# Global value rows of half batches 2 to 5: fetched by one gather and small transfers instead of picked by matmuls

## The chip, the cores and the metric

The kernel runs on one core of one Trainium2 chip. The metric is the device time of one execution in microseconds (us); less is better. The numbers come from a profile of one execution and from three timed runs.

## The reference

Eight batches, eight heads, 576 tokens, head size 64. Each token attends to a band of 32 tokens on either side and to eight global tokens, whose rows and columns are full. The attention output goes through a two-layer network with a cosine gate.

```python
scores = scale * np.matmul(q, k.transpose(0, 1, 3, 2))
mask = np.abs(pos[:, None] - pos[None, :]) <= window          # window = 32
mask = mask | is_global[:, None] | is_global[None, :]
scores = np.where(mask, scores, -1000000000.0)
attn = softmax(scores)                                        # over the last axis
attn_out = np.matmul(attn, v)
x = attn_out.transpose(0, 2, 1, 3).reshape(B * S, H * D)      # 4608 x 512
h = x @ w_in                                                  # 512 x 2048
out = (h * np.cos(h)) @ w_out                                 # 2048 x 512
```

## The kernel before, in words

Work is cut into 16 half batches of four heads, and each of these into two pairs of heads (pair `pr`, 0 to 31). The network is cut into nine blocks of 512 tokens. Every engine runs its instructions in the order in which they are recorded, and that order is written out by hand as strings of steps. `FRONT` covers the first five half batches (pairs 0 to 9) and the first matmuls of the network; `MID`, `FIFTH`, `SIXTH` and `ORDER` cover the rest, in which attention is mixed into the network's matmuls.

In a step's name a digit is a pair or a half batch. In `FRONT`, `k` and `q` turn a pair's keys and queries on TensorE and copy them out on ScalarE (L604, L615, L616); `s` is a pair's scores, exponentials and mask (L631 on TensorE, L634 and L638 on ScalarE, L635 and L639 on VectorE); `p` multiplies with the values and normalizes (L646 on TensorE, L660 to L666 on VectorE); `x` turns the result (L678, L679 to L684); `f` issues filler matmuls that nobody reads (L493); `m` and `t` are the network's first matmuls (L762) and cosines; `n` squares a half batch's result on ScalarE (L818); `H1` turns the gathered global keys and queries on TensorE and copies them on VectorE (L555, L557), and `g` spreads them on GpSimd.

For the first five half batches the values lie in natural layout. `M` clears part of a buffer `vn` on VectorE (L378) and issues five loads from SP's queue (L373), for five windows of 120 rows. Partitions 0 to 7 are kept for the eight global tokens; GpSimd clears them early on (`clear_rows`, L383). `C` casts the buffer to fp16 on GpSimd (L402) into the buffer `vw`, behind a gate, a one-element copy that waits for the mask product of the newest pair recorded so far (L400). `y` then picks a pair's eight global rows out of the cast windows with five matmuls against a 0/1 matrix (L409), and ScalarE copies them into partitions 0 to 7 of all five windows (L410). The buffer of half batch 4 is that of half batch 2, so the clearing of `M4` on VectorE waits for the cast `C2` on GpSimd.

SP's queue numbers its transfers round robin over eight semaphores: a transfer is issued only when the one eight places earlier has landed. GpSimd's queue has its own eight.

Of the kernel before, what the change touches and what calls it, by code (L numbers as in the profile page):

```python
# [17 lines left out]
B, H, S, D = 8, 8, 576, 64  # L18
# [5 lines left out]
G = 8  # L24
# [7 lines left out]
NK5 = 5  # L32
# [9 lines left out]
C = G + QB  # L42
# [10 lines left out]

SIXTH = "sa 2 2 2 2 sz pa 1 1 2 xa pz G 1 1 2 xz n 1 1 D0 2 kc qc D1 1 D2 2 1"

FRONT = ("M1 s0 E0 C0 E1 L2 w6 k1 q1 w4 s1 y0.0 f8 k2 q2 C1 H0 p0 M2 L3 y0.1 s2 k3 q3 f6 x0 p1 M3 H1 g4 g5 g6 C2 y1.0 s3 g7 L4 I k4 q4 f6 x1 p2 M4 y1.1 s4 "
         "C3 W0 k5 q5 f6 x2 p3 y2.0 s5 g8 g9 W1 W2 W3 k6 q6 f6 x3 p4 y2.1 s6 C4 Y0 k7 q7 f6 x4 p5 n0 y3.0 s7 k8 q8 f6 x5 p6 y3.1 s8 H2 k9 q9 f6 x6 p7 y4.0 s9 "
         "x7 p8 y4.1 O m m x8 K5 p9 t t + m m t t x9 -")
WARM = 13
OK_ALL = float(P * (B * NP * 2 * BP + B))  # L60

# [1 line left out]
def view(ap, *dims):  # L63

    return bass.AP(ap.tensor, ap.offset, [ap.ap[0], *[list(d) for d in dims]])


def dview(ap, offset, *dims):

    return bass.AP(ap.tensor, ap.offset + offset, [list(d) for d in dims])  # L70
# [134 lines left out]
def kernel(  # L205
# [10 lines left out]
    nc = tc.nc  # L216
# [46 lines left out]
    def cast_half(s, which):  # L263

        base = s * 4 * S * D
        for x in which:
            if x == "v":
                nc.gpsimd.dma_start(v16[s * 4 * S : (s + 1) * 4 * S].rearrange("(n r) d -> n (r d)", r=16),
                                    dview(v, base, (16 * D, 4 * S // 16), (1, 16 * D)))
            else:  # L270
                src, dst = {"k": (k, k16), "q": (q, q16)}[x]
                nc.gpsimd.dma_start(dst[s].rearrange("t (h d) -> t h d", h=4),  # L272
                                    dview(src, base, (D, S), (S * D, 4), (1, D)))

    def load_qk(s, hs=(0, 4)):

        base = (s * 4 + hs[0]) * S * D
        for src, dst in ((k, kn[s % NN][KPAD : KPAD + S // RW]), (q, qn[s % NN][0 : S // RW])):
            nc.gpsimd.dma_start(dst[:, hs[0] : hs[1]].rearrange("x h r d -> x h (r d)"),
                                dview(src, base, (RW * D, S // RW), (S * D, hs[1] - hs[0]), (1, RW * D)))  # L280
# [9 lines left out]
    vg32 = keep.tile([P, 2, 2, D], FP32)  # L290
# [24 lines left out]
    def warm(n, tag="s"):  # L315

        t = ps.tile([P, 4, P], FP32, tag=tag, bufs=2 + (tag == "s"))
        for _ in range(n):
            nc.tensor.matmul(t, ones16, view(ones16, (0, 4), (1, P)), start=True, stop=True)  # L319

    p8 = keep.tile([P, 1], FP32)
# [10 lines left out]
    def gather(src, dst, half):  # L332
        rows = src.rearrange("b h s d -> (b h s) d")
        for h in range(2):
            nc.gpsimd.indirect_dma_start(
                out=dst[:, half, h], out_offset=None, in_=rows,
                in_offset=bass.IndirectOffsetOnAxis(ap=gidx_rows[:, 0:1], axis=0),
                element_offset=(half * 32 + h) * S * D)
# [23 lines left out]
    def vn_of(s):  # L362
        i = s if s < 4 else 2
        return view(vn32[i // 2][:, 4 * (i % 2)], (4 * D, NK5), (1, 4 * D))

    def load_vn(s, t0=0, t1=NK5):

        rows = vn_of(s)
        for t in range(t0, t1):
            lo = max(KS * t - 24, 0)  # L370
            n = min(KS * t + 96, S) - lo
            p0 = G + (24 if t == 0 else 0)
            nc.sync.dma_start(rows[p0 : p0 + n, t].rearrange("p (h d) -> p h d", h=4),  # L373
                              dview(v, (s * 4 * S + lo) * D, (D, n), (S * D, 4), (1, D)))
# [3 lines left out]
        nc.vector.memset(vn_of(s)[0:64, 0], 0.0)  # L378
        load_vn(s)

    def clear_rows(s):

        nc.gpsimd.memset(vn_of(s)[0:G, 1:], 0.0)  # L383

    gate = keep.tile([1, 1], FP16)

# [367 lines left out]
    def mlp_in(t, f):  # L754
        if f == 0:
            g_of[t] = work.tile([P, NF, TT], FP16, tag="g", name="g")
        g16 = g_of[t]
        tag = "s" if spare[0] and f % 4 > 1 else "h"
        ph = ps.tile([P, TT], FP32, tag=tag, bufs={"s": 3, "h": 2}[tag], name="ph")
        ph_of.append((ph, g16[:, f]))  # L760
        for j in range(NC):
            nc.tensor.matmul(ph, w_in16[:, j, f * P : (f + 1) * P], xT[:, j, t * TT : (t + 1) * TT],  # L762
                             start=(j == 0), stop=(j == NC - 1))

    def mlp_act():
        ph, g = ph_of.pop(0)
        cos = work.tile([P, TT], FP16, tag="cos", bufs=3)
        nc.scalar.activation(cos, ph, AF.Sin, bias=pio2)  # L768
        nc.vector.tensor_tensor(g, cos, ph, ALU.mult)  # L769
# [99 lines left out]
    def one(act=True):  # L869
        for _ in range(1):  # L870

            if ins_q and ins_q[0][0] < ready[0] and ins_q[0][0] < outs_q[0][0] + 2:
                t, f = ins_q.pop(0)
                mlp_in(t, f)
                if act:
                    mlp_act()
                ready[1] = t * NF + f + 1
# [22 lines left out]
    with tc.manual_schedule():  # L900
# [21 lines left out]
        build_band()  # L922
        index_rows(1)
        load_vn(0)
        for s in range(1, 4):
            clear_rows(s)
        load_qk(1)
        build_ones()
        build_mask5()
# [60 lines left out]
            load_values(2 * s)  # L990
            load_values(2 * s + 1)

        def late_gathers(_):

            gather(v, vg32, 0)

        LOCAL = {"k": local_k, "q": local_q}
        OTHER = LOCAL | {"g": globals_kq, "L": load_qk, "W": load_w_in, "v": load_values, "n": x_squares,
                 "C": cast_vn, "I": row_numbers, "E": early_rows, "w": lambda n: warm(n, "h" if n == 6 else "s"), "y": value_rows, "M": next_values, "N": clear_rows, "Y": late_gathers, "V": hold, "U": hold_x, "H": early_globals, "Z": steady_buffers, "f": fill, "r": load_vn, "A": later_rows, "D": later_globals, "O": load_w_out, "K": lambda s: cast_half(s, "vkq"), "B": bring, "m": lambda _: one(False), "t": lambda _: mlp_act()}
        ready[0] = 1  # L1000
        for step in FRONT.split():
            if step in "+-":
                spare[0] = step == "+"
                continue
            f = (STEPS | OTHER)[step[0]]
            f(*[int(x) for x in (step[1:] or "0").split(".")])
        ready[0], front[0] = 2, False
        for s in range(4, B * NP // 2):
            outs_by[0] = 8 * (s - 3)
            for step in {4: MID, 5: FIFTH, 6: SIXTH}.get(s, ORDER).split():  # L1010
# [20 lines left out]
                else:  # L1031
                    f, pr = (STEPS | OTHER)[step[0]], 2 * s + "azcd".index(step[1])
# [56 lines left out]
```

## Time and profile before

| | before |
|---|---|
| median of 3 runs | 351.18 us (351.07 to 353.2) |
| profiled execution | 349.19 us, span 347.3 us |
| TensorE busy | 329.4 us (95%) |
| VectorE busy | 249.5 us (72%) |
| ScalarE busy | 246.0 us (71%) |
| GpSimd busy | 110.0 us (32%) |
| granted TensorE clock, mean | 0.99 |

The span runs from the first to the last instruction; the execution's own time is 1.89 us longer, and its time is 0.6% below the median of the runs. Matmuls overlap, so a busy TensorE is not one at its peak. In the rows below, the time in square brackets is how long an engine stood idle before the instruction, and behind the arrow is what ended the wait. L numbers are lines of the kernel before; the change moves most lines by one.

### The profile page before, as it was taken

To read this page: it belongs to the slowest core of one execution; us is meant where nothing else is said; L and a number is where in the kernel's file an instruction comes from. 1 tells how busy PE (TensorE), PEld (TensorE's weight loads), DVE (VectorE), ACT (ScalarE), POOL (GpSimd) and SP (SyncE) were. 2 spreads that over 40 slices of the span, in tenths; PEclk is the share of its full clock that TensorE was granted. 3 is DMA by queue.
4 is the path that set the end of the run, shared out by engine and by line. 5 is a ranking of instruction groups with operands and counts; after the bars stand their busy time and mean duration, and the time that the engine had idled before them with its cause. 6 is when DMAs were issued, how large, how long until landed. Compare 5 with 4: busy or idle time off the path is not lost.

```text
span 347.3 us, 8464 instructions
## 1 busy us (share of the span) xinstructions
PE 329.4 (95%) x3207; PEld 172.7 (50%) x3207; DVE 249.5 (72%) x611; ACT 246.0 (71%) x423; POOL 110.0 (32%) x221
## 2 busy tenths in 40 slices
PE   7977989999989999999999999999999999999993
PEld 3566865444445454545454545454545344444442
DVE  6665778987597688888797878788888466556310
ACT  8878797796566896878787777878787866644300
POOL 8754846632352506050705062325001000000000
PEclk9999899999999999999999999999999999999997
DMA  5998992999999999999999999999990001100112
GB/s 78 185 165 152 171 195 39 187 175 153 162 153 195 149 155 137 183 150 194 140 171 156 192 142 182 126 219 145 139 134 2 32 30 59 34 31 30 62 60 69
DMA packets 165891, 44.58 MB, mean 128 GB/s; under 512 B 153764, under 2 KB 160996, under 8 KB 165668
## 3 DMA queue, kind: packets, MB, share of 16 engines
q1 hardware_dynamic: 105860, 26.70, 51.5%
q0 software_dynamic: 59984, 17.28, 49.6%
q8 instruction: 27, 0.44, 0.5%
q14 instruction: 20, 0.16, 0.2%
HBM read 44.41 MB, written 19.17 MB: 183 GB/s over the span
## 4 chain that ended last, share of the span: by engine, by line
PE 81%; ACT 6%; DVE 4%; issue 3%; DMA 2%; SPq 1%; POOL 1%; ACTq 0%; POOLq 0%; DVEq 0%
PE po L800 34%; PE ph L762 34%; PE pv L719 3%; PE st L699 3%; PE tx L744 2%; DMA gidx_col<-in_global_idx_dram 1%; ACT e L638 1%; DMA vn<-in_v_dram 1%; PE po L782 1%; PE t L319 1%; PE pv L646 1%; ACT e L634 1%; ACT cos L768 1%; DVE g L769 1%; DVE xn L666 1%
## 5 line engine op out<-in xcount | busy, mean ns | idle before, releaser
L762 PE MATMUL ph<-xT,w_in 128*128 128x512 f16 x576 | 139.3, 379 | 1.1 <-DVE g L769 1.0
L800 PE MATMUL po<-w_out,g 128*128 128x512 f16 x560 | 136.8, 379 | 0.0
L768 ACT ACTIVATE cos<-ph,pio 128x512 f16<-128x512 f32 x144 | 97.0, 687 | 55.3 <-PE ph L762 51.6
L769 DVE TENSOR_TENSOR g<-cos,ph 128x512 f16<-128x512 f16 x144 | 96.5, 685 | 45.6 <-ACT cos L768 43.4
L800 PEld LDWEIGHTS <-g 128*128 128x128 f16 x560 | 53.6, 98 | 63.7
L762 PEld LDWEIGHTS <-w_in 128*128 128x128 f16 x576 | 53.9, 98 | 62.7 <-issue 1.4
L702 ACT ACTIVATE e<-st 128x512 f16<-128x512 f32 x44 | 23.9, 594 | 10.0 <-PE st L699 9.9
L980 POOL COPY gate<-xn 1x1 f16<-1x1 f16 x8 | 1.4, 180 | 81.9 <-DVE xn L730 81.9
L703 DVE TENSOR_TENSOR pm<-e,mask 128x512 f16<-128x512 f16 x44 | 18.7, 425 | 11.7 <-ACT e L702 10.3
L752 POOL COPY xT<-xg 128x4 f16 x48 | 15.4, 320 | 31.5 <-DVE xT L747 28.9
L272 POOL DMA_DIRECT2D q<-in_q_dram x11 | 24.0, 2183 | 0.0
L818 ACT ACTIVATE xn<-xn 128x1536 f16<-128x1536 f16 (+1 forms) x16 | 22.6, 1413 | 0.0
L730 DVE TENSOR_TENSOR xn<-pv,r_all 128x768 f16<-128x768 f32 x22 | 21.1, 957 | 1.0
L805 ACT COPY o<-po 128x512 f32<-128x512 f32 x17 | 10.0, 586 | 14.7 <-PE po L800 14.7
L807 DVE COPY o<-po 128x512 f32<-128x512 f32 x18 | 12.4, 690 | 9.0 <-PE po L800 8.5
L272 POOL DMA_DIRECT2D k<-in_k_dram x11 | 18.1, 1644 | 0.9 <-issue 0.9
L768 ACT ACT_TABLE_LOAD x12 | 15.4, 1283 | 0.2
L702 ACT ACT_TABLE_LOAD x11 | 14.1, 1283 | 0.2
L607 DVE COPY kw<-kT 128x1320 f16<-128x1320 f16 x22 | 13.9, 630 | 0.0
L699 PEld LDWEIGHTS <-kw 64*128 64x128 f16 x484 | 8.4, 95 | 10.7 <-issue 8.1
L579 POOL COPY kw<-kgT 128x88 f16<-128x88 f16 x22 | 12.8, 716 | 0.1
L699 PE MATMUL st<-qb,kw 64*128 64x64 f16 x484 | 11.2, 191 | 1.5 <-DVE qb L619 1.1
(185 smaller groups left out, 391.0 us busy)
## 6 DMA issues: line engine op xcount, KB each, us to landing
out_dram<-o SPq DMA_DIRECT2D x35, 256.0 KB
vw<-v SPq DMA_DIRECT2D x32, 165.0 KB
v<-in_v_dram POOLq DMA_DIRECT2D x11, 288.0 KB, 5.5
k<-in_k_dram POOLq DMA_DIRECT2D x11, 288.0 KB, 8.7
q<-in_q_dram POOLq DMA_DIRECT2D x11, 288.0 KB, 11.5
vn<-in_v_dram SPq DMA_DIRECT2D x20, 120.0 KB
w_in<-in_moe_w_in_dram POOLq DMA_DIRECT2D x4, 512.0 KB, 10.0
w_out<-in_moe_w_out_dram POOLq DMA_DIRECT2D x1, 2048.0 KB, 15.3
```

The lines of the kernel that those rows point to most:

```text
L272: nc.gpsimd.dma_start(dst[s].rearrange("t (h d) -> t h d", h=4), dview(src, base, (D, S), (S * D, 4), (1, D)))
L607: nc.vector.tensor_copy(to, view(kT[pr // 2 % 2][:, pr % 2], (QB, NB), (1, W)))
L699: nc.tensor.matmul(st[j // 8 * 2 + h][:, j % 8 * C : j % 8 * C + C], kp[hp, j], qp[hp, j], start=True, stop=True)
L702: nc.scalar.activation(e[:, 0:512], st[h], AF.Exp, scale=scale)
L703: nc.vector.tensor_tensor(view(pm[:, h], (1, 512)), e[:, 0:512], view(mask, (1, 512)), ALU.mult)
L730: nc.vector.tensor_tensor(view(xn, (384, 2), (D, 6), (1, D)), view(pv, (512, 2), (65, 6), (1, D)), view(rp, (6, 2), (1, 6), (0, D)), ALU.mult)
L752: nc.gpsimd.tensor_copy(xT[:, :, bass.ds(pool_idx[g] + b * S, 1)], xg[:, :, g : g + 1])
L762: nc.tensor.matmul(ph, w_in16[:, j, f * P : (f + 1) * P], xT[:, j, t * TT : (t + 1) * TT], start=(j == 0), stop=(j == NC - 1))
L768: nc.scalar.activation(cos, ph, AF.Sin, bias=pio2)
L769: nc.vector.tensor_tensor(g, cos, ph, ALU.mult)
L800: nc.tensor.matmul(po, g16[:, f, s * P : (s + 1) * P], w_out16[:, f], start=(f == 0), stop=(f == NF - 1))
L818: nc.scalar.activation(view(xn, (BP * P, 2), (1, n)), view(xn, (BP * P, 2), (1, n)), AF.Square, accum_out=x_sq[:, s : s + 1])
```

## The change

The eight `y` steps of half batches 1 to 4 are taken out: 40 picking matmuls and eight copies on ScalarE. Half batch 0 keeps its two. The gather of the global value rows into `vg32`, two indirect transfers that stood behind `C4`, now stands before the loads of half batch 1's keys and queries, where the three clearings of `clear_rows` were. For each pair 2 to 9 a step `S` issues one transfer on SP's queue from `vg32` into partitions 0 to 7 of all five windows of `vn`, behind the loads of `M`; the cast `C` then takes them along. Eight `f6` become `f4`, and `s3` is moved ahead of `H1 g4 g5 g6 C2`.

```diff
-FRONT = ("M1 s0 E0 C0 E1 L2 w6 k1 q1 w4 s1 y0.0 f8 k2 q2 C1 H0 p0 M2 L3 y0.1 s2 k3 q3 f6 x0 p1 M3 H1 g4 g5 g6 C2 y1.0 s3 g7 L4 I k4 q4 f6 x1 p2 M4 y1.1 s4 "
-         "C3 W0 k5 q5 f6 x2 p3 y2.0 s5 g8 g9 W1 W2 W3 k6 q6 f6 x3 p4 y2.1 s6 C4 Y0 k7 q7 f6 x4 p5 n0 y3.0 s7 k8 q8 f6 x5 p6 y3.1 s8 H2 k9 q9 f6 x6 p7 y4.0 s9 "
-         "x7 p8 y4.1 O m m x8 K5 p9 t t + m m t t x9 -")
+FRONT = ("M1 S2 S3 s0 E0 C0 E1 L2 w6 k1 q1 w4 s1 y0.0 f8 k2 q2 C1 H0 p0 M2 S4 S5 L3 y0.1 s2 k3 q3 f4 x0 p1 M3 S6 S7 s3 H1 g4 g5 g6 C2 g7 L4 I k4 q4 f4 x1 p2 M4 S8 S9 s4 "
+         "C3 W0 k5 q5 f4 x2 p3 s5 g8 g9 W1 W2 W3 k6 q6 f4 x3 p4 s6 C4 k7 q7 f4 x4 p5 n0 s7 k8 q8 f4 x5 p6 s8 H2 k9 q9 f4 x6 p7 s9 "
+         "x7 p8 O m m x8 K5 p9 t t + m m t t x9 -")
-    def clear_rows(s):
-        nc.gpsimd.memset(vn_of(s)[0:G, 1:], 0.0)
+    def spread_vg(pr):
+        nc.sync.dma_start(vn_of(pr // 2)[0:G, :, 2 * D * (pr % 2) : 2 * D * (pr % 2 + 1)],
+                          view(vg32[pr * G : (pr + 1) * G, 0], (0, NK5), (1, 2 * D)))
...
         load_vn(0)
-        for s in range(1, 4):
-            clear_rows(s)
+        gather(v, vg32, 0)
         load_qk(1)
```

How the instructions stand now, at three places. First SP's queue from the last load of half batch 1 (buffer `vn_117`) to the first loads of half batch 3 (`vn_118` holds half batches 2 and 3). Before:

```order
L373 DMA vn_117<-in_v_dram 120x4x64 [waits DMAHW4_49]
L373 DMA vn_118<-in_v_dram 96x4x64 [waits DMAHW5_49,DVE_49]
L373 DMA vn_118<-in_v_dram 120x4x64 [waits DMAHW6_49]
L373 DMA vn_118<-in_v_dram 120x4x64 [waits DMAHW7_49]
L373 DMA vn_118<-in_v_dram 120x4x64 [waits DMAHW0_49]
L373 DMA vn_118<-in_v_dram 120x4x64 [waits DMAHW1_49]
L373 DMA vn_118<-in_v_dram 96x4x64 [waits DMAHW2_49,DVE_49]
```

With the change:

```order
L373 DMA vn_117<-in_v_dram 120x4x64 [waits DMAHW4_49]
L383 DMA vn_117<-vg_106 8x5x128 [waits DMAHW5_49,DMASW5_49,DMASW4_49]
L383 DMA vn_117<-vg_106 8x5x128 [waits DMAHW6_49]
L373 DMA vn_118<-in_v_dram 96x4x64 [waits DMAHW7_49,DVE_49]
L373 DMA vn_118<-in_v_dram 120x4x64 [waits DMAHW0_49]
L373 DMA vn_118<-in_v_dram 120x4x64 [waits DMAHW1_49]
L373 DMA vn_118<-in_v_dram 120x4x64 [waits DMAHW2_49]
L373 DMA vn_118<-in_v_dram 120x4x64 [waits DMAHW3_49]
L383 DMA vn_118<-vg_106 8x5x128 [waits DMAHW4_49]
L383 DMA vn_118<-vg_106 8x5x128 [waits DMAHW5_49]
L373 DMA vn_118<-in_v_dram 96x4x64 [waits DMAHW6_49,DVE_49]
```

Two small transfers stand behind each half batch's five loads. The first of all also waits for the gather (the two DMASW semaphores).

Second, GpSimd around the gate and the cast `C2` of half batch 2 (`vw_94<-vn_118`). Before:

```order
L577 COPY kw_98<-kgT 128x5x8 [waits PE_49,Activation_49]
L584 COPY qb_102<-qgT 128x4x8 [waits Activation_49]
L400 COPY gate<-pm 1x1
L402 CAST vw_94<-vn_118 128x20x64 [waits DMAHW5_49,DMAHW6_49,DMAHW1_49,DMAHW7_49,DMAHW0_49,Pool_49]
L577 COPY kw_99<-kgT 128x5x8 [waits PE_49,Activation_49]
```

With the change:

```order
L578 COPY kw_98<-kgT 128x5x8 [waits PE_49,Activation_49]
L585 COPY qb_102<-qgT 128x4x8 [waits Activation_49]
L401 COPY gate<-pm 1x1
L403 CAST vw_94<-vn_118 128x20x64 [waits DMAHW4_49,DMAHW3_49,DMAHW5_49,DMAHW2_49,DMAHW7_49,DMAHW1_49,DMAHW0_49]
L578 COPY kw_99<-kgT 128x5x8 [waits PE_49,Activation_49]
```

The cast waits for seven transfers instead of five: the five loads and the two small ones.

Third, ScalarE from the squares of half batch 0 (`x_sq`) to pair 9's exponentials. Before:

```order
L818 ACTIVATE xn,x_sq<-xn 128x2x640
L410 CAST vw_95<-rows 8x5x2x64
L634 ACTIVATE e<-st 128x488 x2
L638 ACTIVATE e<-st 128x384 x2
L604 COPY kw_96<-bank 128x5x120
L615 COPY qb_100<-bank 128x8
L616 COPY qb_100<-bank 128x5x120
L410 CAST vw_95<-rows 8x5x2x64
L634 ACTIVATE e<-st 128x488 x2
```

With the change:

```order
L819 ACTIVATE xn,x_sq<-xn 128x2x640
L635 ACTIVATE e<-st 128x488 x2
L639 ACTIVATE e<-st 128x384 x2
L605 COPY kw_96<-bank 128x5x120
L616 COPY qb_100<-bank 128x8
L617 COPY qb_100<-bank 128x5x120
L635 ACTIVATE e<-st 128x488 x2
```

The copies of the picked rows are gone; nothing else on ScalarE has changed places here.

More of the change, by code (lines that the diff above doesn't have):

```diff
@@ L991, in bring @@
             load_values(2 * s + 1)
-        def late_gathers(_):
-            gather(v, vg32, 0)
         LOCAL = {"k": local_k, "q": local_q}
         OTHER = LOCAL | {"g": globals_kq, "L": load_qk, "W": load_w_in, "v": load_values, "n": x_squares,
-                 "C": cast_vn, "I": row_numbers, "E": early_rows, "w": lambda n: warm(n, "h" if n == 6 else "s"), "y": value_rows, "M": next_values, "N": clear_rows, "Y": late_gathers, "V": hold, "U": hold_x, "H": early_globals, "Z": steady_buffers, "f": fill, "r": load_vn, "A": later_rows, "D": later_globals, "O": load_w_out, "K": lambda s: cast_half(s, "vkq"), "B": bring, "m": lambda _: one(False), "t": lambda _: mlp_act()}
+                 "C": cast_vn, "I": row_numbers, "E": early_rows, "w": lambda n: warm(n, "h" if n == 6 else "s"), "y": value_rows, "M": next_values, "S": spread_vg, "V": hold, "U": hold_x, "H": early_globals, "Z": steady_buffers, "f": fill, "r": load_vn, "A": later_rows, "D": later_globals, "O": load_w_out, "K": lambda s: cast_half(s, "vkq"), "B": bring, "m": lambda _: one(False), "t": lambda _: mlp_act()}
         ready[0] = 1
```

## The prediction

> **What bounds the kernel now.** I read the busy times by stage first, then the chain of waits inside the stage that the change touches, then single engines in order of time.
>
> ```profile
> 0.00:20.00 20.00, 17.11 (x297) 9.88 (x298) 12.02 (x59) 16.79 (x34) 15.22 (x27) 1.00 0.88 132
> 20.00:33.00 13.00, 10.09 (x256) 8.64 (x257) 8.16 (x26) 10.41 (x26) 6.22 (x15) 1.00 1.02 177
> 33.00:36.40 3.40, 1.91 (x51) 1.40 (x50) 3.33 (x13) 2.78 (x6) 2.99 (x5) 1.00 0.58 105
> 36.40:39.90 3.50, 3.50 (x45) 3.06 (x42) 2.36 (x9) 1.36 (x4) 2.62 (x7) 0.51 1.02 165
> 39.90:57.20 17.30, 15.07 (x304) 11.81 (x299) 13.51 (x44) 16.65 (x35) 9.35 (x27) 1.00 0.88 143
> 57.20:347.30 290.10, 281.71 (x2274) 137.85 (x2273) 210.11 (x464) 197.95 (x322) 73.57 (x144) 0.99 1.04 125
> ```
>
> The columns are length, busy TensorE, weight loads, VectorE, ScalarE, GpSimd, granted clock, DMA share and GB/s. From 57.2 us on TensorE is busy 97%, and the change touches nothing there. So the change is worth what it moves the end of the front, at about 57 us, and all that follows moves along with it. In the front no engine is the bound throughout: up to 33 us a wait for transfers decides, from 39.9 on ScalarE (16.65 of 17.30).
>
> The wait is in the chain:
>
> ```profile
> 20.60 0.28 DVE vn L378
> 20.89 0.32 SPq L373
> ...
> 22.84 3.53 DMA vn<-in_v_dram
> ...
> 26.51 0.35 POOL gate L400
> 26.87 4.57 issue
> ...
> 31.56 1.26 POOL vw L402
> ...
> 32.93 0.27 DVE vn L378
> ```
>
> `M2` clears its buffer at 20.60 and SP issues half batch 2's loads from 20.89 on. GpSimd passes the gate at 26.9, and then the cast `C2` stands still until 31.56. The chain calls these 4.57 us "issue"; by the program's order the cast waits there for the five loads and nothing else. VectorE, which has come to `M4`'s clearing, waits for the cast:
>
> ```profile
> 27.65 0.56 DVE L639 TENSOR_TENSOR pm<-e,qT 128x768 f16<-128x768 f16 x1 [0.35 <-ACT e L638]
> ...
> 29.20 0.82 DVE L666 TENSOR_TENSOR xn<-pv,r_all 128x640 f16<-128x640 f32 x1
> 32.93 0.27 DVE L378 MEMSET vn<- 64x256 f32 x1 [2.90 <-POOL vw L402]
> ...
> 35.25 0.82 DVE L666 TENSOR_TENSOR xn<-pv,r_all 128x640 f16<-128x640 f32 x1
> ```
>
> After it VectorE has pair 4's mask, pair 2's transposes and pair 3's normalization to catch up on, in one piece until 36.07, and TensorE waits for that (1.91 busy of 3.40 us). So whatever the change saves before 30 us ends in this wait. The transfers are busy meanwhile:
>
> ```profile
> 27.00:31.00 4.00, 3.72 (x91) 3.26 (x89) 2.60 (x9) 4.00 (x10) 0.00 (x0) 1.00 1.23 219
> 31.00:34.00 3.00, 1.67 (x32) 1.18 (x28) 1.07 (x4) 1.94 (x6) 2.44 (x3) 1.00 0.36 68
> ```
>
> At 219 GB/s up to 31 us and 68 after it, the loads end just where the cast starts.
>
> **Part by part: what leaves.** In this part TensorE and ScalarE stand as follows.
>
> ```profile
> 36.13 0.81 PE L493 MATMUL pv<-ones 128*128 128x184 f16 x6 [0.26 <-DVE xn L666]
> 37.27 1.59 PE L646 MATMUL pv<-vw,pm 128*128 128x65 f16 x20
> 38.67 0.72 PE L409 MATMUL rows<-vw,one_v 128*8 128x128 f16 x5
> 39.32 0.79 PE L631 MATMUL st<-qb,kw 64*128 64x136 f16 x10
> ```
>
> ```profile
> 39.43 0.69 ACT L410 CAST vw<-rows 8x640 f16<-8x640 f32 x1 [2.14 <-PE rows L409]
> 40.02 1.01 ACT L634 ACTIVATE e<-st 128x488 f16<-128x488 f32 x2
> ...
> 42.83 1.27 ACT L818 ACTIVATE xn<-xn 128x1280 f16<-128x1280 f16 x1
> ...
> 44.10 0.67 ACT L410 CAST vw<-rows 8x640 f16<-8x640 f32 x1
> 44.67 1.02 ACT L634 ACTIVATE e<-st 128x488 f16<-128x488 f32 x2
> ...
> 46.93 0.64 ACT L616 COPY qb<-bank 128x600 f16<-128x600 f16 x1
> 47.50 0.69 ACT L410 CAST vw<-rows 8x640 f16<-8x640 f32 x1
> 48.13 1.04 ACT L634 ACTIVATE e<-st 128x488 f16<-128x488 f32 x2
> ```
>
> *Pair 6* (`y2.1`): pair 4's value matmuls end at 38.86; the five picks push the scores back to 39.32, and ScalarE, free since 37.29 (the 2.14 us of idling), starts the exponentials at 40.02, 0.70 later. Without picks, and with two fillers fewer (0.81/6 each, 0.27 in all), the scores start at 38.86 - 0.27 = 38.59 and the exponentials at 39.29: **0.73 us** gained. *Pair 7* (`y3.0`): ScalarE is busy without a gap from 40.02 on and the scores are done since 43.54 (next fence), so the copy's place, 44.10 to 44.67, is gained: **0.57**. *Pairs 8 and 9* (`y3.1`, `y4.0`): here the copy lies in a hole. The query copy L616 ends at 47.57, the scores need it, and
>
> ```profile
> 42.99 0.55 PE L631 MATMUL st<-qb,kw 64*128 64x136 f16 x10 [0.18 <-ACT qb L616]
> ...
> 47.72 0.55 PE L631 MATMUL st<-qb,kw 64*128 64x136 f16 x10 [0.26 <-ACT qb L616]
> ```
>
> the exponentials cannot start before about 48.13 with the copy or without it. I take **0.05** for each of the two. `y4.1` comes after the last exponentials and nobody waits for it: 0. The cover is the round trip over TensorE; were it gone, each copy would be worth its 0.6.
>
> *Before 30 us* (`y1.0`, `y1.1`, `y2.0`, the moved `s3`): `s3` no longer waits for the copies of `H1`,
>
> ```profile
> 25.44 0.53 PE L631 MATMUL st<-qb,kw 64*128 64x136 f16 x9 [1.04 <-DVE kgT L557]
> ```
>
> so VectorE reaches `M4` about 1.3 us earlier (1.04 and part of the picks) and waits that much longer for `C2`. Worth 0 while the stall covers it, 1.3 without it. The gate of `C2` now stands for pair 3's mask instead of pair 2's, which is ready at 28.21 (L639 above) in the trace as it is; the loads still come later.
>
> **What is added.** `C2` now waits for `S4` and `S5`, behind the five loads in SP's queue. The trace has no such transfer in the front; the nearest are the 8-partition spreads of later pairs, and the gathers:
>
> ```profile
> L414 SPq DMA_DIRECT2D vw<-vg x44: 685/714/2304, 80.6 to 254.5; - x44
> L335 POOL DMA_INDIRECT vg<-in_v_dram,gidx_rows x4: 952/1018/1164, 45.8 to 74.0; - x4
> ```
>
> One spread moves 8 x 5 x 512 bytes, 20 KB. From below: 40 KB at 219 GB/s are 0.18 us. From above: two at the median issue time of 0.714 are 1.43. I take 0.5, nearer to the bytes, since SP has idle time between `M2` and `M3`. A gain is possible too: `C1` waits for `S2` and `S3` in the same way, the load of half batch 3's keys stands behind `C1` on GpSimd, and issued 0.5 later it shares less with half batch 2's values. I put the lower end at -0.5. The first `S` holds SP until the gather has landed; behind it are only `M2`'s loads, at 20.9, and the gather is issued near 6 us.
>
> The two gathers take 2 x (0.30 + 1.02) = 2.64 us of GpSimd in place of three clearings of together 2.75, but wait for the index rows,
>
> ```profile
> 5.89 0.16 DVE L330 SCALAR_TENSOR_TENSOR gidx_rows<-p,gidx_col 128x1 int32<-128x1 f32 x1 [0.28 <-DMA gidx_col<-in_global_idx_dram]
> 5.62 2.75 POOL L383 MEMSET vn<- 8x1024 f32 x3
> ```
>
> so half batch 1's keys are issued about 0.4 us later, behind 64 KB of gathered rows. `q2` runs at 17.5, close to where its queries land; the delay reaches `M2` and hence `C2` between 0 and 0.5: I take 0.2. The gathers taken out at 45.8 free GpSimd where it had time.
>
> **Sum.** -0.73 - 0.57 - 0.10 + 0.5 + 0.2 = -0.7 us. Against the profiled execution, 349.19, that is 348.5. The median of the runs is 351.18, and with the same step I forecast **350.5**. From the bounds of the unknown costs (-0.5 to 1.43, 0 to 0.5) its own range is 349.3 to 351.7.
>
> **Rivals.** *The stall goes.* If the later `C1` keeps half batch 3's keys out of the way of half batch 2's values, the cast is ready when VectorE comes. Then the stall's 2.90 us is gained beside the 1.40, less 0.2: 347.1. For it: the DMA share of 1.23 while the cast waits. Against: the keys would have to be issued some 3 us later, and their queue is backed up anyway.
>
> *ScalarE is the bound throughout.* Eight copies at 0.686 each are 5.5 us; less 0.7, 346.4. For it: 16.65 busy of 17.30. Against: the holes at 47.6 and 51.1.
>
> ```profile
> L410 ACT CAST vw<-rows 8x640 f16<-8x640 f32 x10 | 6.9, 686 | 5.4 <-PE rows L409 5.4
> ```
>
> *The cast comes later (slower).* `S4` and `S5` sit last in the queue that `C2` waits for; at the longest row (2.304 each) the cast comes 4.6 us later, every gain behind it starts from there, and the time is 351.18 + 4.6 + 0.2 - 1.4 = 354.6. It turns the change into a loss from 1.2 us of delay on. For it: they are the last to land by construction. Against: SP has nothing else to issue just then. The Trainium skill (DMA: Bandwidth & Descriptors, Rules for kernel authors) says that an outermost dimension below 16 confines a transfer to so many engines, which speaks for this rival, since these have 8; no run here shows the engines one by one.
>
> *The clock drops (slower).* After the stall the granted clock stood at 0.51 for 3.5 us, following 1.91 us of work in 3.40. There one pair's value matmuls took 1.59 us; at full clock:
>
> ```profile
> 41.49 1.03 PE L646 MATMUL pv<-vw,pm 128*128 128x65 f16 x20
> ```
>
> With picks, scores and turns, each about half as long again, I estimate 1.5 us a pair. The change takes 16 fillers and 40 picks away, TensorE's slack grows, and three more such stretches on the path would give 351.18 + 4.5 - 0.7 = 355.0. Against: from 39.9 on TensorE is busy 15.07 of 17.30, and losing some 0.6 us a pair leaves it far above the 1.91 of 3.40. The Trainium skill (TensorE: Matmul & The Clock Gate, Part 1) has the clock halved after an idle window of about 3.4 us; by that rule the new work here would not trip it after 39.9, and the trace's one drop, after a stretch that was half busy, came earlier than the rule's wording.
>
> **How the numbers follow.** Forecast 0.50; stall goes 0.17 (0.14 of it over 1%); ScalarE throughout 0.08; later cast 0.15 (0.06 of it over 1%); clock 0.10 (0.06 over 1%). One per cent is 3.5 us, about what a measurement of this kernel can tell from no change. Faster 0.14 + 0.08 = 0.22, slower 0.12, the rest, 0.66, within. The range is 346.8 to 353.4: it takes in the first rival, and leaves out the second and the far ends of the two slower ones.
>
> **What would show it.** Right: `C2` starts near 32 us again, `M4`'s clearing waits longer than 2.90, pair 6's exponentials start near 39.8, and pairs 7 to 9 follow with 4.1, 3.5 and 3.5 us between them instead of 4.65, 3.46 and 3.54. Wrong: `C2` starts before 30 or after 33 us, or the granted clock drops again after 40.

## The result, and the profile after

The changed kernel takes 350.21 us (median of 12 runs, 347.95 to 354.19); the kernel before, run beside it, 351.25 (12 runs). The ratio is 0.9943, with a 95% interval of 0.9915 to 0.9971. Here and below the ratios leave disturbed runs out, while the medians keep them. The forecast was 350.5, with 0.66 on a change within 1%, and that is what came. The size is less sure: the forecast gain was 0.7 us, and the ratio stands for 2.0 us in this set of runs and for 0.8 in a second one. The way to the number was partly another one, and that it came so near is partly luck, since two errors cancelled.

Stages of the changed kernel, with the columns of the first table of the prediction:

```profile
20.00:33.00 13.00, 9.56 (x253) 7.98 (x248) 9.03 (x30) 10.07 (x26) 6.67 (x15) 1.00 1.08 174
33.00:36.40 3.40, 2.34 (x55) 2.14 (x54) 3.33 (x12) 2.55 (x7) 2.12 (x6) 0.88 0.80 129
36.40:39.90 3.50, 3.50 (x69) 2.88 (x66) 2.47 (x10) 2.02 (x5) 3.41 (x7) 0.63 1.17 192
39.90:57.20 17.30, 14.31 (x247) 10.17 (x244) 14.59 (x48) 13.76 (x28) 10.34 (x26) 1.00 0.89 145
57.20:347.30 290.10, 279.39 (x2259) 137.12 (x2256) 208.29 (x459) 196.56 (x320) 70.80 (x142) 1.00 1.08 125
```

From 39.9 to 57.2 us ScalarE is down from 16.65 us to 13.76 and TensorE from 15.07 to 14.31; since the changed kernel is ahead by then, the stretch also holds some work that came after it before. What happened ahead of it is in the timeline of GpSimd, of SP's queue (SPq: start, and how long SP needed to issue them all) and of VectorE:

```profile
16.65 1.60 SPq L383 DMA_DIRECT2D vn<-vg  x2
...
23.06 1.25 POOL L403 CAST vw<-vn 128x1280 f16<-128x1280 f32 x1 [4.48 <-DMA vn<-vg]
...
23.73 2.08 SPq L383 DMA_DIRECT2D vn<-vg  x2
...
24.73 0.71 POOL L279 DMA_DIRECT2D kn<-in_k_dram  x1
...
30.51 1.25 POOL L403 CAST vw<-vn 128x1280 f16<-128x1280 f32 x1 [2.30 <-DMA vn<-vg]
...
31.88 0.27 DVE L378 MEMSET vn<- 64x256 f32 x1 [2.49 <-POOL vw L403]
```

`C1` waits for the small transfers of half batch 1 and starts at 23.06 instead of 20.06. Half batch 3's keys stand behind it on GpSimd, so they are issued at 24.73 instead of 22.09. `C2` starts at 30.51 instead of 31.56, now waiting for its own small transfers: by the semaphore events of the trace its five loads have landed by 28.1 (before: 31.4) and `S5` by 30.3. `M4`'s clearing waits 2.49 us instead of 2.90. Then TensorE and ScalarE from pair 4's fillers to pair 9:

```profile
35.08 0.48 PE L494 MATMUL pv<-ones 128*128 128x184 f16 x4 [0.92 <-DVE xn L667]
...
35.74 1.59 PE L647 MATMUL pv<-vw,pm 128*128 128x65 f16 x20
...
37.88 1.04 ACT L635 ACTIVATE e<-st 128x488 f16<-128x488 f32 x2 [2.33 <-PE st L632]
...
41.97 1.09 ACT L635 ACTIVATE e<-st 128x488 f16<-128x488 f32 x2
...
45.52 1.04 ACT L635 ACTIVATE e<-st 128x488 f16<-128x488 f32 x2 [0.50 <-PE st L632]
...
49.02 1.04 ACT L635 ACTIVATE e<-st 128x488 f16<-128x488 f32 x2 [0.50 <-PE st L632]
```

Pair 6 starts 2.14 us earlier (37.88 against 40.02). The steps to pairs 7, 8 and 9 are 4.09, 3.55 and 3.50 us, against 4.65, 3.46 and 3.54. At the network's first regular cosine (the first one of an even stream, one every 0.86 us) the lead is 2.61 us; before:

```profile
61.20 0.69 ACT L768 ACTIVATE cos<-ph,pio 128x512 f16<-128x512 f32 x1 [0.17 <-PE ph L762]
```

after:

```profile
58.59 0.69 ACT L769 ACTIVATE cos<-ph,pio 128x512 f16<-128x512 f32 x1 [0.17 <-PE ph L763]
```

Of that, 2.1 us were lost again between 97 and 119 us and most of the rest later, so this one execution ends where the one before ended (span 347.3 both).

### The profile page after: what moved, and what is told of

It reads as the page before. It is cut to its first block, busy times and chain, and to the rows that moved or that the text cites. A ratio compares the mean times of both kernels' runs of the same rounds, so it can differ in the third digit from the quotient of the medians.

```text
span 347.3 us, 8353 instructions
## 1 busy us (share of the span) xinstructions
PE 325.7 (94%) x3153; PEld 170.1 (49%) x3153; DVE 249.0 (72%) x611; ACT 241.5 (70%) x415; POOL 108.4 (31%) x218
## 4 chain that ended last, share of the span: by engine, by line
PE 72%; DMA 8%; DVE 5%; SPq 4%; ACT 3%; issue 3%; POOL 3%; POOLq 0%; ACTq 0%; DVEq 0%
PE ph L763 30%; PE po L801 30%; DMA q<-in_q_dram 3%; PE pv L720 3%; PE st L700 2%; PE tx L745 2%; DVE g L770 2%; DMA vn<-vg 2%; DMA kn<-in_k_dram 2%; DMA vw<-vg 1%; ACT cos L769 1%; PE po L783 1%; SPq L415 1%; POOL w_in L894 1%; PE pv L647 1%
## 5 line engine op out<-in xcount | busy, mean ns | idle before, releaser
L635 ACT ACTIVATE e<-st 128x488 f16<-128x488 f32 x20 | 10.5, 578 | 7.2 <-PE st L632 5.5
L720 PE MATMUL pv<-vw,pm 128*64 128x65 f16 x484 | 13.0, 197 | 1.1 <-DMA vw<-vg 0.8
```

Of the source, the lines that this page charges most:

```text
L720: nc.tensor.matmul(pv[r0 : r0 + C, j // 6, c0 : c0 + 65], pm[:, h, j], vp[:, j, h], start=True, stop=True)
```

## The experiments

The theory after the comparison (T): what is handed to the transfers ahead of half batch 3's keys decides when `C2` starts; the late keys brought it forward, the small transfers behind the loads took part of that back. A second one (K) came up on the way: less work on TensorE brings more stretches at half clock. All kernels ran in 12 executions beside the kernel before (the eleventh in one). The four sets of runs (1 to 4, 5 to 8, 9 to 11, and 12) ran on four chips, so across the sets the ratios compare and the medians do not. The times of `C2` and pair 6 are those of one trace each. Kernel 5 leaves the global value rows of half batch 2 out of the result, and kernel 7 those of half batches 1 to 4.

| kernel | median, us | before beside it | ratio (95%) | granted clock, median of the runs | `C2` | pair 6 |
|---|---|---|---|---|---|---|
| the change | 350.21 | 351.25 | 0.9943 (0.9915 to 0.9971) | 0.986 | 30.51 | 37.88 |
| 1 again | 350.19 | 351.25 | 0.9976 (0.9943 to 1.0009) | 0.9845 | 29.67 | 37.54 |
| 2 keys ahead of `C1` | 351.46 | 351.25 | 1.0009 (0.9975 to 1.0042) | 0.979 | 32.40 | 40.21 |
| 3 small ones ahead of loads | 352.24 | 351.25 | 1.0025 (0.9994 to 1.0056) | 0.982 | 33.80 | 41.60 |
| 4 before, keys late | 349.47 | 351.25 | 0.9966 (0.9943 to 0.9989) | 0.992 | 28.71 | 37.41 |
| 5 without `S4`, `S5` | 351.18 | 351.84 | 0.9998 (0.9946 to 1.0051) | 0.985 | 28.58 | 40.43 |
| 6 refilled | 350.74 | 351.84 | 0.9945 (0.9914 to 0.9976) | 0.992 | 31.05 | 38.03 |
| 7 before, no copies | 351.44 | 351.84 | 0.9977 (0.995 to 1.0004) | 0.988 | 31.59 | 40.58 |
| 8 small ones early, refilled | 351.64 | 351.84 | 1.0001 (0.9971 to 1.003) | 0.987 | 32.56 | 40.73 |
| 9 change, keys later | 350.35 | 350.7 | 0.9997 (0.9963 to 1.0032) | 0.983 | 28.46 | 38.21 |
| 10 the same, refilled | 352.44 | 350.7 | 1.0031 (0.9989 to 1.0073) | 0.9855 | 29.08 | 40.66 |
| 12 ninth with idle work | 351.16 | 351.61 | 0.9979 (0.9945 to 1.0013) | 0.989 | 29.38 | 39.56 |

The clock's median of the kernel before was 0.9885, 0.987, 0.986 and 0.9895 in the four sets.

### 1. The change again

No edit.

> The changed kernel unchanged, a second profiled execution. In the first, C1 started at 23.06 us, C2 at 30.51, pair 6's exponentials at 37.88, and the network's stream at 56.73, 2.6 earlier than before; of that lead 2.4 us were gone by 150 us. If the front is set by the transfers as I read it, the front comes again: C1 at 22.6 to 23.4, C2 at 30.1 to 30.9, pair 6 at 37.5 to 38.3. Theory A (the transfers at 100 to 118 us do not move with the engines): the lead again falls from over 2 us to under 0.8 between 100 and 120 us, and the time in the fast runs is 0.1 to 0.7 us below before. Theory B (that loss was one execution's own): the lead is above 1.5 us at the end, and the fast runs are 1.5 to 2.6 us below before (ratio 0.993 to 0.996).

`C1` at 22.12 and `C2` at 29.67 were a little earlier than the ranges, pair 6 inside its own. The clock was not the same; busy time by stretch:

```profile
20.28:23.69 3.41, 2.25 (x82) 2.08 (x76) 2.32 (x7) 3.08 (x9) 1.57 (x2) 1.00 1.13 182
23.69:30.51 6.82, 6.28 (x93) 4.95 (x89) 4.29 (x20) 3.14 (x8) 3.70 (x12) 0.50 1.14 179
47.58:50.99 3.41, 1.41 (x25) 0.99 (x25) 3.34 (x12) 2.89 (x7) 0.12 (x1) 1.00 1.24 207
50.99:54.41 3.42, 3.42 (x21) 1.54 (x18) 2.22 (x8) 1.46 (x2) 1.91 (x9) 0.50 0.46 78
```

Three half-clock stretches of 3.4 us instead of one left a lead of 1.1 us at the first regular cosine (60.11). It lost next to nothing of that later: the span is 346.4. So theory A falls as it was put: the loss at 97 to 119 us does not come with the change every time. Theory B's numbers were not reached either, since this front led by 1.1 and not by 2.6.

### 2. Half batch 3's keys ahead of `C1`

```diff
-... k2 q2 C1 H0 p0 M2 S4 S5 L3 ...
+... k2 q2 L3 C1 H0 p0 M2 S4 S5 ...
```

> The change with one step moved: half batch 3's keys and queries are issued ahead of the cast C1 on GpSimd instead of behind it, so near 18.6 us instead of 24.73. Theory T (the late C1 keeps these keys out of the way of half batch 2's values; the two small transfers behind those cost about 2 us): the values' five loads land at 31 or later again, S5 after them, C2 starts at 31.5 to 33, M4's clearing waits 3.5 us or more, pair 6's exponentials start at 39 to 40.3, and the time is 1 to 2.5 us above the change. Rival R1 (the keys' time does not matter to C2; it came earlier for another reason, such as GpSimd's or SP's own order): C2 within 0.4 of 30.5 and the time within 0.6 us of the change.

GpSimd, and SP's queue:

```profile
19.08 0.75 POOL L279 DMA_DIRECT2D kn<-in_k_dram  x1
...
21.01 5.67 SPq L373 DMA_DIRECT2D vn<-in_v_dram  x5
...
32.40 1.25 POOL L403 CAST vw<-vn 128x1280 f16<-128x1280 f32 x1 [4.12 <-DMA vn<-in_v_dram]
```

Everything in T's ranges: `C2` at 32.40, pair 6 at 40.21, the median 1.3 us above the change. (A part of the time may be the clock's: this trace has three half-clock stretches in a row from 34.9 us on.) The loads landed by 31.65 and `S5` by 32.17. R1 falls.

### 3. The small transfers ahead of the loads

```diff
         nc.vector.memset(vn_of(s)[0:64, 0], 0.0)
+        if s > 1:
+            spread_vg(2 * s)
+            spread_vg(2 * s + 1)
         load_vn(s)
```

(and `S4` to `S9` taken out of `FRONT`)

> The change with the two small transfers of half batches 2, 3 and 4 issued ahead of the five loads instead of behind them. Theory T (S5 is the last to land, 2.2 us after the loads, and only for its place): S4 and S5 land by 25, the loads by 28.5 to 29.3, C2 starts at 28.6 to 29.4, M4's clearing waits under 1.3 us, pair 6's exponentials start at 36.3 to 37.0, and the front ends about 1.2 us earlier than in the change. Rival R2 (the transfers are bound by what moves in all, the order only says who waits): the loads land at 30 or later and C2 within 0.4 of 30.5. Rival R3 (small transfers hold the queue up): SP needs over 2 us for the two, the loads come later still, C2 after 31.

```profile
20.80 1.42 SPq L386 DMA_DIRECT2D vn<-vg  x2
...
22.25 3.76 SPq L373 DMA_DIRECT2D vn<-in_v_dram  x5
...
24.71 0.71 POOL L279 DMA_DIRECT2D kn<-in_k_dram  x1
...
33.80 1.25 POOL L406 CAST vw<-vn 128x1280 f16<-128x1280 f32 x1 [4.45 <-DMA vn<-in_v_dram]
```

I expected the gain and got R3's number, `C2` at 33.80. But R3's reason is not it: SP needed 1.42 us for the two, and they had landed by 24.2. The last two loads were issued at 24.98 and 25.51, behind the keys at 24.71, and landed at 31.75 and 33.56. So my reading that `S5` was late "only for its place" behind its loads was wrong. The two loads that came last are those that went out behind the keys. Why SP needed 1.63 us to issue the load ahead of them, instead of some 0.5, stays open.

### 4. The kernel before with late keys

```diff
-... p0 M2 L3 y0.1 ... x0 p1 M3 ...
+... p0 M2 y0.1 ... x0 p1 U1 L3 M3 ...
```

(`U1` is a one-element copy on GpSimd that waits for pair 1's normalization)

> The kernel before with one thing changed: half batch 3's keys and queries wait on GpSimd for pair 1's normalization, so are issued near 25.2 us instead of 22.09. Picks, copies and fillers stay. Theory T: half batch 2's loads land near 28.1 instead of 31.36, C2 starts at 28.1 to 28.9 instead of 31.56, M4's clearing waits under 0.5 us instead of 2.90, pair 6's exponentials start near 37.1 to 37.9 instead of 40.02, and the front ends 2 to 2.9 us earlier, all without the change's gather and small transfers. Rival R1: C2 stays at 31.2 or later, and the time within 0.5 us of before. Rival R4 (the keys, now late, become the next wait): C2 comes early but pair 6 waits for its keys on TensorE, and the front is not earlier by more than 0.5 us.

```profile
25.80 0.72 POOL L279 DMA_DIRECT2D kn<-in_k_dram  x1 [0.36 <-issue]
...
28.58 0.18 POOL L400 COPY gate<-pm 1x1 f16<-1x1 f16 x1
28.71 1.25 POOL L402 CAST vw<-vn 128x1280 f16<-128x1280 f32 x1
...
30.23 0.27 DVE L378 MEMSET vn<- 64x256 f32 x1
...
34.30 0.47 PE L595 MATMUL bank<-ident,qn 76*64 76x76 f16 x16 [0.81 <-DMA qn<-in_q_dram]
...
37.41 1.01 ACT L634 ACTIVATE e<-st 128x488 f16<-128x488 f32 x2
```

T holds: one moved load, no early gather, all picks and copies in place, and `C2` comes 2.85 us earlier, the wait of `M4`'s clearing is gone, pair 6 starts 2.61 us earlier, and the runs are 0.34% faster (0.9943 to 0.9989). That is about what the whole change brings. The loads had landed by 27.8, and the cast starts right behind its gate: from here on the mask that the gate waits for sets `C2`, and no longer the transfers.

### 5. The change without `S4` and `S5`

```diff
-... M2 S4 S5 ...
+... M2 ...
+        clear_rows(2)
         gather(v, vg32, 0)
```

> The change without the two small transfers of half batch 2: its global value rows are cleared early on GpSimd and left out of the sum, so pairs 4 and 5 lack their global values. C1 and the keys stay late. Theory T (S5 is what the cast waits for last): C2 starts when the five loads have landed and the gate is passed, at 28.1 to 29.0 us instead of 30.51; M4's clearing waits under 0.8 us; pair 6's exponentials start at 36.2 to 37.2 unless the granted clock is halved on the way. Rival R2 (what moves in all decides): C2 at 30 or later. On the clock, theory K: with the stall gone TensorE's idlest 3.4 us in the front are busier, so fewer halvings, and the median of the runs' mean granted clock is above the change's 0.9845 to 0.986.

```profile
26.14 0.71 POOL L279 DMA_DIRECT2D kn<-in_k_dram  x1
...
28.58 1.25 POOL L407 CAST vw<-vn 128x1280 f16<-128x1280 f32 x1
...
36.72 0.50 PE L600 MATMUL bank<-ident,qn 76*64 76x76 f16 x16 [2.22 <-DMA qn<-in_q_dram]
```

`C2` as expected, 28.58, right behind its gate (28.46). That does not yet show what `S5` costs, since the keys also went out 1.4 us later than in the change; the ninth run has `S4` and `S5` and about the same `C2`. Pair 6 was not as expected: the keys went out at 26.14, their queries landed at 36.7, TensorE stood for them, the clock halved, and pair 6 came at 40.43. So the wait had moved on to the transfer that gave way.

### 6. TensorE refilled

```diff
-... g6 C2 g7 ... x0 ... s4 ... (f4 throughout)
+... g6 C2 F g7 ... x0 ... F s4 ... (f6 throughout, F where each y stood)
+    def stand_in(_):
+        t = ps.tile([P, 512], FP32, tag="h", bufs=2, name="stand")
+        for _ in range(NK5):
+            nc.tensor.matmul(t[0:G, 0 : 2 * D], one_v[:, 0], ones16, start=True, stop=True)
```

> The change with TensorE's work put back: f6 instead of f4, and in the place of each taken-out pick five matmuls of the same size against the ones, which wait for nothing and which nobody reads. The small transfers, the late keys and ScalarE without copies stay. In the six traces so far, the granted clock fell to one half for the next 3.4 us wherever TensorE was busy 66% or less of a 3.4 us stretch, and stayed full from 67% up. Theory K (the change's missing work brings more stretches under that share): the median of the runs' mean granted clock returns to 0.988 or more (before: 0.9885; the change: 0.9845 to 0.986), pair 6's exponentials come up to 0.8 us later than in a run of the change at the same clock, and the median of the runs is 0.3 to 1.2 us below the change's 350.2. Rival R5 (the clock's halvings come from the stall alone and the fillers do not matter): clock at 0.983 to 0.986 and the median 0.4 to 1.0 us above the change.

The clock came back, 0.992. The time did not follow: by the ratios beside before it is 0.9945 against 0.9943 and 0.9976. Here K is right on the clock, and it is not shown on the time.

### 7. The kernel before without ScalarE's copies

```diff
-        nc.scalar.copy(vn16(s)[0:G, :, hs, 0:D], ...)
+        if s == 0:
+            nc.scalar.copy(vn16(s)[0:G, :, hs, 0:D], ...)
```

> The kernel before without ScalarE's eight copies of half batches 1 to 4, whose global value rows are therefore left out; picks, fillers, clearings, transfers and order stay. By my prediction's terms: nothing before 40 us (C2 at 31.2 to 31.9, pair 6's exponentials at 39.7 to 40.1), then 4.1 us to pair 7 instead of 4.65, 3.5 to pair 8 and to pair 9 as before; the front 0.5 to 0.8 us earlier, the runs 0.3 to 0.9 us below before. Rival (ScalarE is the bound throughout): the gaps are 4.0, 2.9 and 2.9, the front 1.8 to 3 us earlier, and the time down by as much.

```profile
40.58 1.04 ACT L635 ACTIVATE e<-st 128x488 f16<-128x488 f32 x2 [3.11 <-PE st L632]
...
44.66 1.09 ACT L635 ACTIVATE e<-st 128x488 f16<-128x488 f32 x2
...
48.95 1.05 ACT L635 ACTIVATE e<-st 128x488 f16<-128x488 f32 x2 [1.25 <-PE st L632]
```

The step to pair 7 is 4.08 us, as forecast; `C2` is unmoved at 31.59. Pair 6 came late, with the clock halved for 6.8 us here instead of 3.4. The step to pair 8 was 4.29, not the 3.5 forecast: ScalarE waited 1.25 us for the scores, and why those came late stays open. The ratio is 0.9977, and its interval includes 1. So a worth of the copies beyond the noise is not shown, and ScalarE as the bound throughout falls, since it asked for steps of 2.9 to pairs 8 and 9.

### 8. Small transfers early, refilled

```diff
-... M1 S2 S3 s0 E0 ... M2 S4 S5 ... M3 S6 S7 ...
+... M1 S2 S3 s0 S4 S5 S6 S7 E0 ... M2 ... M3 ...   (refilled as in 6)
```

> A version meant to beat both: the change refilled as in the run before, and the small transfers of half batches 2 and 3 issued right behind those of half batch 1 (near 18 to 21 us, ahead of half batch 2's loads; the top 32 rows are cleared earlier for it), so that no cast waits for one behind its loads. Theory T and K together: C1 at 22.5 to 24, keys of half batch 3 at 24 to 26, C2 at 28.1 to 29.3, M4's clearing waits under 0.8 us, pair 6's exponentials at 36.8 to 37.8, mean granted clock 0.988 or more, and the runs 2.5 to 3.5 us below before (347.7 to 348.7). Rival R3 (small transfers ahead of loads hold the queue, as they did in the third experiment, where C2 came at 33.80): C2 after 30.5 and the runs no better than the change.

```profile
21.53 11.23 SPq L373 DMA_DIRECT2D vn<-in_v_dram  x10
...
24.63 0.71 POOL L279 DMA_DIRECT2D kn<-in_k_dram  x1
...
32.56 1.25 POOL L412 CAST vw<-vn 128x1280 f16<-128x1280 f32 x1 [3.77 <-DMA vn<-in_v_dram]
```

A miss, and as in the third run by a load that went out behind the keys: the fifth load of half batch 2 was issued at 25.32, with the keys at 24.63, and landed at 32.41. What held it is the rule of SP's eight semaphores: eight places earlier stands `S4`, which landed at 25.30 by the semaphore events.

### 9 and 10. The change with later keys, bare and refilled

```diff
-... M2 S4 S5 L3 y0.1 ... x0 p1 M3 ...
+... M2 S4 S5 y0.1 ... x0 p1 U1 L3 M3 ...
```

> The change with half batch 3's keys and queries held on GpSimd until pair 1 is normalized (near 25.7 us instead of 24.73), so that S5 is issued wholly ahead of them. Theory T (what is issued to the transfers ahead of these keys decides C2): the loads and S4, S5 land by 28.8, C2 starts at 28.4 to 29.3 instead of 30.51, M4's clearing waits under 1.2 us, pair 6's exponentials start at 36.3 to 37.3 with one half-clock stretch on the way, and the median of the runs is 0.3 to 1.5 us below the change's 350.2. Rival R4 (the queries, now later, are the next wait): TensorE stands over 1 us before pair 6's queries, pair 6 at 38 or later, and the runs no better than the change. Rival (S5 is late whatever stands behind it): C2 at 30 or later.

> The same with TensorE refilled as before: f6, and five idle matmuls in the place of each pick. Theories T and K together: C2 at 28.4 to 29.3, pair 6's exponentials at 36.8 to 37.8, the median of the runs' mean granted clock 0.990 or more, and the runs 2 to 3.5 us below before (ratio 0.990 to 0.995), the best of the versions. If only T holds, the clock is 0.984 to 0.987 and the runs lie with the run before this one. If the queries are the next wait (R4), pair 6 comes at 38 or later and the ratio is above 0.995.

The ninth:

```profile
25.44 0.72 POOL L279 DMA_DIRECT2D kn<-in_k_dram  x1
...
28.46 1.26 POOL L403 CAST vw<-vn 128x1280 f16<-128x1280 f32 x1 [0.50 <-DMA vn<-vg]
...
29.83 0.27 DVE L378 MEMSET vn<- 64x256 f32 x1 [1.05 <-POOL vw L403]
...
34.44 0.67 PE L596 MATMUL bank<-ident,qn 76*64 76x76 f16 x16 [1.95 <-DMA qn<-in_q_dram]
...
38.21 1.04 ACT L635 ACTIVATE e<-st 128x488 f16<-128x488 f32 x2 [2.34 <-PE st L632]
```

its busy time by stretch:

```profile
31.11:34.53 3.42, 0.93 (x28) 0.56 (x26) 2.91 (x11) 2.36 (x5) 1.97 (x6) 1.00 1.22 201
34.53:37.94 3.41, 3.41 (x51) 3.03 (x53) 0.79 (x5) 0.73 (x2) 0.00 (x0) 0.50 1.35 180
```

and the tenth:

```profile
35.90 0.72 PE L602 MATMUL bank<-ident,qn 76*64 76x76 f16 x16 [2.37 <-DMA qn<-in_q_dram]
```

T's half on `C2` holds in both (28.46, 29.08; the tenth's cast starts right behind its gate at 28.93). R4 takes the other half: TensorE stands 1.95 and 2.37 us for half batch 3's queries, and the clock halves behind that. By the ratios (0.9997 and 1.0031) neither is better than the change. K missed in the tenth: refilled, its clock was 0.9855, where 0.990 or more was expected.

### 11. The kernel before again

No edit; one run, 350.55 us.

> The kernel before unchanged, a second profiled execution, to see how far one execution's front stands for others: C1 at 19.7 to 20.4, C2 at 31.2 to 31.9, one half-clock stretch after C2's stall, the network's stream at 58.8 to 60.0 us. If the front varies by more than 1 us without a difference in the half-clock stretches, front times of single traces cannot carry differences of that size.

`C1` at 19.95, `C2` at 31.29, one half-clock stretch from 35.8 on, the network's stream at 59.25: all in their ranges. The first regular cosine is at 61.17 against 61.20. With the clock's stretches alike, the front repeats within 0.3 us at `C2` and 0.03 at its end, so single traces can carry differences of 1 us and more. With other stretches they cannot: the change's own two traces differ by 0.84 at `C2` and by 1.5 at the first regular cosine. And behind the front this trace loses 1.4 us to the first one, between 136 and 214 us, though the two kernels are the same.

### 12. The ninth with idle work

```diff
-... k6 q6 f4 ... p7 s9 x7 ...
+... k6 w6 q6 f4 ... p7 s9 F x7 ...
```

> The ninth experiment's kernel (change, keys of half batch 3 held to 25.4 us) with idle work in two of TensorE's waits: six matmuls of 512 columns between pair 6's keys and queries, where TensorE stood 1.95 us for the queries, and five small ones behind pair 9's scores. The ninth ran at a median clock of 0.983 with halvings at 34.5 and 51.6, its pair 6 came at 38.21 and its runs at 350.35. Theory K (what is left is lost to halvings, which follow 3.4 us stretches with TensorE busy 66% or less): no halving between 31 and 42 in the trace, pair 6's exponentials at 36.5 to 37.2 although the queries land as late as before, the clock's median 0.988 or more, and the runs 1.0 to 2.5 us below those 350.35. Rival R4 alone (only the wait for the queries counts): pair 6 at 37.8 to 38.8, clock 0.981 to 0.985, the runs within 0.8 us of the ninth's.

```profile
24.11 1.25 POOL L409 CAST vw<-vn 128x1280 f16<-128x1280 f32 x1 [5.80 <-DMA vn<-in_v_dram]
...
26.34 0.23 PE L562 MATMUL t<-ident,g 128*128 128x128 f16 x1 [1.98 <-POOL g L539]
```

The clock's median rose from 0.983 to 0.989, as K has it, but the traced execution lost its clock elsewhere, from 28.6 to 35.4, behind another wait: `C1` came at 24.11, the casts for `H1` stand behind it on GpSimd, and TensorE waited 1.98 us for them (there was no such wait in the first trace of the change). So a late `C1` can have a price of its own. Pair 6 at 39.56 and the runs at 351.16 miss what K expected; that refilling wins time is not shown by any of the refilled kernels (6, 8, 10 and 12).

## Why the prediction was right, and which steps were wrong

**Right:** the parts behind 36 us. Pair 7's term was 0.57, measured 0.56 and, with the copies alone taken out, 0.57. Pairs 8 and 9: a gain of 0.05 each was forecast, and the two steps together came out 0.05 longer (7.05 against 7.00), so nothing was gained. ScalarE from 39.9 on looked like the bound and was not, since the copies to pairs 8 and 9 lay in the round trip over TensorE. The gather's 0.2 was about right too: `M2`'s loads went out at 21.25 instead of 20.89, and at 20.95 in the second trace. Pair 6's 0.73 measured 1.09 (the 2.14 less the 1.05 of `C2`): 0.61 for the picks, from the end of the values to the exponentials (1.16 before, 0.55 after), and 0.48 from the start of the fillers to the values (1.14, 0.66). I had 0.46 and 0.27. What goes beyond them is at least in part the clock's: the fillers (35.08) now end as the halving begins (35.6), and before they began at 36.13 and ran into it (36.4).

**Wrong, a term of the sum with the wrong sign:** "I take 0.5" for `S4` and `S5`, with 0.2 for the gathers, put `C2` 0.7 later; it came 1.05 earlier, beyond even the lower end of -0.5. The step that failed is the size of `C1`'s delay. Three signs that I had set for being right failed with it: `C2` was not near 32, `M4`'s clearing did not wait longer than 2.90, and pair 6 did not start near 39.8 (the fourth, steps of 4.1, 3.5 and 3.5 to pairs 7 to 9, came); in the second trace two signs of being wrong came, `C2` before 30 (29.67) and a halving after 40 us (at 51.0). I named the mechanism (`C1` waits, the keys stand behind it) but let `C1` come 0.5 later, and it came 3.0 later, since `S3`, issued at 17.54, lands at 22.91 by the semaphore events. The keys went out 2.64 us later, the "some 3 us" that I had set as the condition of the rival *the stall goes*, and had held unlikely. Across the traces, issue of the keys and start of `C2`: 19.08 and 32.40; 21.85, 31.59; 21.99, 31.29; 22.09, 31.56; 24.04, 29.67; 24.67, 31.05; 24.73, 30.51; and 28.46 to 29.38 for keys at 25.44 to 26.92. That is a trend between three groups and no more. Within the middle group the earliest keys have the earliest cast, and in the last group the transfers no longer decide: in runs 4, 5, 10 and 12 the cast starts 0.12 to 0.15 us after its gate. The two kernels off this order, 33.80 and 32.56 with the keys at 24.71 and 24.63, had two or four small transfers more ahead of the loads, so that loads went out behind the keys. The Trainium skill (DMA: Bandwidth & Descriptors, Issuing engines are not separate DMA queues) says that queues of different engines use the same DMA engines and interleave there; the runs agree, for GpSimd's keys and SP's values.

**The rival *the stall goes* was half right:** its cause came and a part of its effect. Its price, the whole 2.90, is bounded by the next wait, as runs 5, 9 and 10 show: with `C2` at 28.5 to 29.1, half batch 3's queries hold TensorE for 1.95 to 2.37 us. It is not too high everywhere: in run 4 the queries cost 0.81, and pair 6 came 2.61 earlier.

**The rival *the clock drops* came in part.** The trace of the result has one half-clock stretch in the front like before; the second has three, and led by 1.1 us instead of 2.6. The median clock is 0.9845 to 0.986 against 0.986 to 0.9895. Refilled, the sixth kernel is at 0.992, the eighth at 0.987 and the tenth at 0.9855, so what refilling does to the clock is not settled. In the second trace TensorE was busy 1.41 of 3.41 us ahead of the halving at 51 us: I had put its slack there too far from the point where the clock falls.

**Wrong: that everything behind 57 us moves along.** In the first trace 2.1 of 2.6 us were lost at 97 to 119, where TensorE is busy 17.64 us of 21:

```profile
97.00:118.00 21.00, 17.64 (x171) 9.07 (x170) 15.73 (x36) 13.72 (x25) 9.60 (x19) 1.00 1.28 157
101.21 0.67 PE L700 MATMUL st<-qb,kw 64*128 64x64 f16 x22 [2.18 <-DVE qb L620]
```

in the kernel before 19.72:

```profile
97.00:118.00 21.00, 19.72 (x204) 9.94 (x203) 17.28 (x40) 14.69 (x27) 10.80 (x20) 1.00 1.53 174
```

and in the second trace 19.70, with nothing lost:

```profile
97.00:118.00 21.00, 19.70 (x201) 9.94 (x201) 17.35 (x41) 14.08 (x27) 11.64 (x23) 1.00 1.60 156
```

Measured against the first trace of before, the traces lose between 0 and 3.5 us there: the second of before 0, the fourth run (before, keys late) 0.3, the seventh (before, no copies) 0.7, the second and third (variants of the change) 3.5 and 3.0. Of the ten traces with the change or a variant, six lose 1.7 us or more there, and of the four of the kernel before and its variants none loses over 0.7. So the loss may still belong to the change in some way. What sets it from one execution to the next stays open. So does the size of the gain, 0.57% in one set of runs and 0.24% in the other. That it is real rests on the first interval, and on the order of the table: the four rows whose pair 6 starts by 38.1 us have ratios of 0.9943 to 0.9976, the eight later ones 0.9977 to 1.0031. That border was drawn after the fact, though, and the ninth, with 38.21 and 0.9997, lies just behind it. No version was shown to be faster than the change. The fourth, which needs none of its parts, cannot be told from it.

## What to carry to other kernels

When a step gets a new wait, list what stands behind it on its engine, the transfers above all: here 1.05 us of the 2.65 that pair 9 came earlier are due to a load that was issued 2.6 us later, and moving such a load alone (run 4) gained what cannot be told from the whole change's gain. Whether a moved transfer pays is limited by the transfer that yields: in three kernels a wait of up to 2.9 us went, and one of 2 us for the yielding queries came up. And before taking idle work off TensorE, look how empty its emptiest 3.4 us stretches become; that refilling them wins time is not shown here.

## What the runs showed of the hardware

The granted clock fell to one half, for 3.4 us at a time, behind stretches of the same length in which TensorE was busy between 11 and 60%, so not idle. In the fronts of fourteen traces all 16 full-clock stretches of 3.4 us with TensorE busy 60% or less were followed by half clock, 2 of 7 between 61 and 67%, and one above (73%). Between 97 and 230 us, among the network's matmuls, stretches busy 49 to 61% were followed by it only once in 7, so the busy share alone is not the whole rule. The Trainium skill (TensorE: Matmul & The Clock Gate, Part 1) has the clock drop after an idle window of about 3.4 us in a free-running grid; the length agrees, the idleness does not: 1.91 us of work in 3.40 was enough for a drop.

A transfer of 20 KB over 8 partitions needs not be slow: ahead of the loads two were issued in 1.42 us and had landed 3.4 us after the first was issued. After a first event on its semaphore each had eight more at its landing, where a load of 120 rows had fifteen; that alone did not make it slow. Behind the loads, `S5` took 5.8 us (24.48 to 30.28) with the keys issued 0.25 us after it. In the ninth run, with the keys 0.28 us after it, it took 3.1 (25.16 to 28.23), so a place just ahead of the keys does not by itself make it slow either.
